# Two PSUM banks of an attention and mixture-of-experts kernel: one tile of two banks, or a tile each

## Chip, cores and metric

One core of a Trainium2 chip. The metric is the device time of one execution in microseconds (us). A measurement of this kernel can tell about 0.5% from no change.

## What is computed

Attention with random features for 4 batches, 8 heads and 576 positions gives x (2304 tokens by 512). A mixture of eight experts with Sinkhorn-balanced gates follows, and then one wide expert with a swish:

```python
out = np.zeros((N, D))                       # N = 2304, D = 512
for e in range(8):                           # first layer, F = 1024
    h = np.maximum(x @ w1[e], 0.0)
    out += P[:, e:e + 1] * (h @ w2[e])       # P: gates, 8 rounds of row and column scaling
h = out @ w_in                               # second layer, F = 2048
g = h * (1.0 / (1.0 + np.exp(-1.702 * h)))
result = g @ w_out
```

## The kernel before

The kernel first runs attention (some 210 us) and then 60 *visits*. A visit takes one block of 768 tokens (j = 0, 1, 2) through one pair of hidden chunks of 256 (c = 0, 1). There are 16 pairs of the first layer (8 experts of 2), 48 visits, and 4 pairs of the second, 12 visits. Products are made of seven smaller ones each (Strassen's scheme), and each fp32 number is two operands, a rounded one and the remainder, so a product is three matmuls.

- **Up** (`up_fast`, L1145): seven products a chunk on banks 0 to 4 and on bank 7 (`q`), six matmuls of 384 columns each (L1157), 84 in a visit. ScalarE (L1167) and VectorE (L1178, L1189, L1216) read the sums out of PSUM and form fourteen operands `h`, rounded and remainder; some of the remainders are made by GpSimd (L395).
- **Down** (`down`, L1288): DOWN (L1263) lists seven products, TURNS (L1273) their order as (n, c), PLACES (L1282) the bank and half bank of each of three token tiles t. A turn is three groups of three matmuls of 256 columns (L1302), 126 in a visit. C sits in bank 5 (both halves) and the first half of 6, E in bank 7 (both halves) and the second half of 6, D in banks 0, 2 and 1. After a turn with c = 1 the three sums are read: VectorE adds each to `acc` (L1328, L1335), or ScalarE copies it (L1318, L1324).

The two are interleaved: `all_visits` (L1383) takes the first turn of down, then the rest of up's second chunk, then the other turns; the last turn falls into the next visit. The order of the turns in both layers, the order of the token tiles t in a turn, and the banks:

```python
TURNS: (0,0), (0,1), (3,0), (1,0), (1,1), (2,0), (2,1), (3,1), (4,0), (4,1), (5,0), (5,1), (6,0), (6,1)
order = (0, 1, 2) if c == 0 else (0, 2, 1) if n == 3 else (2, 0, 1)
PLACES = {"C": ((5, 0), (5, 1), (6, 0)), "D": ((0, 0), (2, 0), (1, 0)), "E": ((7, 0), (7, 1), (6, 1))}
```

`rec` and `plan.add` (L62) collect every operation with its engine, a cost and the keys that it reads and writes. `Plan.run` (L112) then plays them through and fixes one order for each engine; an operation comes behind the last writer of each key that it touches, and a writer behind its readers too. Banks have the keys ("b", 0) to ("b", 7), one each. TensorE's main operations keep the order in which they were recorded. After that the operations are issued in this order, and semaphores between the engines are put in for each tile that two of them touch.

PSUM has eight banks of 512 fp32 columns. Banks 0 to 5 are tiles of their own. Banks 6 and 7 are the halves of one tile, PAIR (L362), because attention reads its sums of all eight heads from both banks with one instruction (`kv_step` L599, `attend` L644, `divide` L656, key PAIRS). The experts use them as `bank[6]` and `bank[7]`, views of PAIR. In the profile all that touches either of them has the name `pair`.

Of the kernel before, what the change touches and what calls it, by code (L numbers as in the profile page):

```python
# [10 lines left out]
F32 = mybir.dt.float32  # L11
# [5 lines left out]
PSUM = bass.MemoryType.PSUM  # L17
# [176 lines left out]
def tile_performer_sinkhorn_moe(  # L194
# [14 lines left out]
    nc = tc.nc  # L209
# [3 lines left out]
    E, _, F = w1.shape  # L213
    F2 = w_in.shape[1]
    P = 128
# [16 lines left out]
    Q = SUP // 2  # L232
# [3 lines left out]
    psum = ctx.enter_context(tc.tile_pool(name="psum", bufs=1, space=PSUM))  # L236
    dram = ctx.enter_context(tc.tile_pool(name="dram", bufs=1, space=bass.MemoryType.DRAM))
    plan = Plan()
# [13 lines left out]
    T = {}  # L252
# [18 lines left out]
    n = 0  # L271
# [21 lines left out]
    lg = part(SIG, "sig", 0, NTILE * E, "lg").rearrange("p (t e) -> p t e", e=E)  # L293
# [27 lines left out]
    n = H * M  # L321
# [31 lines left out]
    n = 16 * Q  # L353
# [5 lines left out]
        n += NP * P  # L359
    plan.share()  # L360

    PAIR = psum.tile([P, 2, 512], F32, name="pair")  # L362
    bank = {i: psum.tile([P, 512], F32, name=f"bank{i}") for i in range(6)}
    bank[6], bank[7] = PAIR[:, 0, :], PAIR[:, 1, :]

    scr_in = dram.tile([NC2, P, NK, FC], F32, name="scr_in")
    scr_out = dram.tile([NC2, P, NF, DM], F32, name="scr_out")
# [36 lines left out]
    def act(dur, fn, r, w):  # L404
        rec("ACT", dur, lambda e: fn(), r, w)

    def dve(dur, fn, r, w):
        rec("DVE", dur, lambda e: fn(), r, w)
# [188 lines left out]
    PAIRS = [("b", 6), ("b", 7)]  # L597

    def kv_step(b, t, f, first, last):  # L599
# [3 lines left out]
        def fn():  # L603
            for h in range(H):
                nc.tensor.matmul(
                    PAIR[:, h // 4, (h % 4) * VW : (h % 4) * VW + D + 1], f[r, h, :], vv[r, h, 0 : D + 1],
                    start=first and h % 4 == 0, stop=last, skip_group_check=True,
# [3 lines left out]
        if last:  # L611
# [4 lines left out]
                    t.rearrange("p (a h) w -> p a h w", a=2)[:, :, :, 0 : D + 1],  # L616
                    PAIR[:, :, 0 : 4 * VW].rearrange("p a (h w) -> p a h w", w=VW)[:, :, :, 0 : D + 1],
                    AF.Copy, scale=1.0 / M,
# [25 lines left out]
    def attend(ft, b):  # L644
        (ft, kf), (kx, kk) = ft, kvs[b]

        def fn():
            for h in range(H):
                nc.tensor.matmul(
                    PAIR[:, h // 4, (h % 4) * VW : (h % 4) * VW + D + 1], ft[:, h, :], kx[:, h, 0 : D + 1],  # L650
                    start=True, stop=True,
# [4 lines left out]
    def divide(x, rows):  # L656
        x, kx = x
        n = rows.stop - rows.start
        nv = PAIR[:, :, 0 : 4 * VW].rearrange("p a (h w) -> p a h w", w=VW)
        den, kd = little("den")  # L660
        rd, kr = little("rd")
        den, rd = (y.rearrange("p (a h w) -> p a h w", a=2, w=1) for y in (den, rd))
        V = nc.vector
        dve(
            0.2,
            lambda: V.tensor_scalar(
                out=den[rows], in0=nv[rows, :, :, D : D + 1], scalar1=1e-6, scalar2=None, op0=ALU.add
            ),
            PAIRS, [kd],
        )  # L670
        dve(0.2, lambda: V.reciprocal(out=rd[rows], in_=den[rows]), [kd], [kr])
        dve(
            0.69,
            lambda: V.tensor_tensor(
                out=x[rows].rearrange("p (a h d) -> p a h d", a=2, h=4), in0=nv[rows, :, :, 0:D],
                in1=rd[rows].to_broadcast([n, 2, 4, D]), op=ALU.mult,
            ),
            PAIRS + [kr], [kx],
        )
# [23 lines left out]

    def logits(j, half, b):

        lp, kp = bank[b], ("b", b)
        first, second = ((0, wg, 0), (3, wg, 2)) if half == 0 else ((1, wg, 0), (6, wgd, 0))
        n = ST // 2

        def fn():  # L710
            for a in range(2):
                for m, (o, w, at) in enumerate((first, second)):
                    for kk in range(2):
                        nc.tensor.matmul(
                            lp[0 : (2 - a) * E, :Q], w[:, at + kk, 0 : (2 - a) * E], T["xo"][o][:, a, kk],
                            start=a + m + kk == 0, stop=m + kk == 2, skip_group_check=True,
                        )

        pe(8 * MM, fn, [("xo", first[0]), ("xo", second[0]), "wg", "wgd"], [kp])
        if j == 0:  # L720
            lt, kt = T["spare"][6 + half], [("spare", 6 + half)]
        else:
            lt, kt = T["stage"][:, half * 2 * FC : half * 2 * FC + Q], [("stage", 2 * half), ("stage", 2 * half + 1)]
        act(0.5, lambda: nc.scalar.copy(lt[0 : 2 * E], lp[0 : 2 * E, :Q]), [kp], kt)

        def back():
            for t in range(n):
                nc.tensor.transpose(
                    lp[:, t * 2 * E : (t + 1) * 2 * E], lt[0 : 2 * E, t * P : (t + 1) * P],
                    ident[0 : 2 * E, 0 : 2 * E],  # L730
                )

        pe(3 * 0.11, back, kt, [kp], main=False)
        o = ST * j + n * half
        dve(
            0.3,
            lambda: nc.vector.tensor_reduce(
                out=lg[:, o : o + n, :], in_=lp[:, 0 : n * 2 * E].rearrange("p (t s e) -> p t e s", s=2, e=E),
                op=ALU.add, axis=AX.X,
            ),  # L740
            [kp], [("lg", j, half)],
        )
# [6 lines left out]
    def attention():  # L749

        seq = []
        for b in range(B):
            seq += [("k", b, t) for t in range(NT + (b + 1) % 2)]
            seq += [("q", b, t) for t in range(NT + b % 2)]
        n = len(seq)
        ins, xs = {}, {}

        def at(i, what):
            return 0 <= i < n and seq[i][0] in what

        for s in range(-5, n + 3):
            if s == n - 2:
                turn["ps"] = [4, 5]
                plan.add("X", 0.0, lambda e: switch(), (), [k for _, k in slots["b2"]] + H_KEYS)
            if at(s + 5, "kq"):
                squares(*seq[s + 5])
            if at(s + 4, "kq"):
                ins[s + 4] = project_in(*seq[s + 4])
            if at(s, "q"):
                ft = transpose_q(feat.pop(s))  # L770
            if at(s + 2, "kq"):
                pj = features(*ins.pop(s + 2))
                w, b, t = seq[s + 2]
                if w == "k" and t == NT:
                    f = ktail[b // 2] = KTAIL, "ktail"
                else:
                    i = taken("f4")
                    f = F4[i], ("f4", i)
                feat[s + 2] = f
                exps(*pj, sums.pop(seq[s + 2]), f)  # L780
            yield s - n, 0
            if at(s, "q"):
                _, b, t = seq[s]
                attend(ft, b if t < NT else b - 1)
            if at(s, "k"):
                _, b, t = seq[s]
                f = feat.pop(s)
                last = seq[s + 1][0] == "q"
                kv_step(b, t, f, t == 0, last and b % 2 == 0)
                if last and b % 2 == 1:  # L790
                    kv_step(b, NT, ktail.pop(b // 2), False, True)
            if at(s, "q"):
                _, b, t = seq[s]
                x = slot(DM, kind="sq")
                divide(x, slice(0, P if t < NT else TAIL))
                xs[s] = x
            yield s - n, 1
            if at(s - 1, "q"):
                j, t = divmod(PLACE[token_tile(*seq[s - 1][1:])], ST)
                transpose_x(xs.pop(s - 1), j, t)  # L800
            yield s - n, 2
            if at(s - 2, "q"):
                j, t = divmod(PLACE[token_tile(*seq[s - 2][1:])], ST)
                if t == ST - 1:
                    x_operands(j)
            yield s - n, 3
            if at(s, "q") and seq[s][2] == NT:
                attend(ft, seq[s][1])
                divide(x, slice(TAIL, 2 * TAIL))
            if 1 <= s < n - 8:  # L810
                load_tile(*seq[s + 8])
            if 4 <= s and at(s + 5, "k"):
                load_tile("v", *seq[s + 5][1:])
# [641 lines left out]
    with tc.manual_schedule():  # L1455
        setup()
        for t in range(NT):
            load_tile("k", 0, t)
        load_tile("k", 0, NT)
        for what, t in (("v", 0), ("v", 1), ("q", 0), ("v", 2), ("q", 1), ("v", 3), ("v", NT), ("q", 2), ("q", 3)):  # L1460
            load_tile(what, 0, t)
        load_gate()
        for c in range(2):
            prepare(0, "w1", c, 0)
            split("w1", c, 0)
        prepare(0, "w2", 0, 0)
        visits = all_visits()
        for at in attention():
            if at in EARLY:
                take(visits)  # L1470
        for _ in visits:
            pass
        for e, o in plan.run():
            o.fn(ENGINES.get(e))
        h_pool.close()


# [28 lines left out]
```

## Time and profile before

| what | value |
| --- | --- |
| device time, median of 3 runs | 2240.61 us (2237.18 to 2249.94) |
| the profiled execution: device time | 2244.87 us |
| the profiled execution: span, first to last instruction | 2243.1 us |
| mean granted TensorE clock | 0.987 |
| busy in the span: TensorE matmuls / weight loads | 2081.2 us (93%) / 1987.6 us (89%) |
| busy in the span: VectorE / ScalarE / GpSimd | 65% / 48% / 56% |

The profile is of one execution. PE is TensorE's matmuls, PEld its weight loads, DVE VectorE, ACT ScalarE, POOL GpSimd, SP the engine that issues the DMAs; L1302 is a line of the kernel. Matmuls overlap and their ends are modelled. "Idle before" is the time that an engine stood still ahead of an instruction, with what ended the wait.

### The profile page before, as it was taken

Reading aid. Unit: us, or ns where it says so; the run is one execution under the profiler, and the core shown is the slowest. Engines: PE = TensorE matmul, PEld = TensorE weight load, DVE = VectorE, ACT = ScalarE, POOL = GpSimd, SP = SyncE. Lnnn points to the kernel's source line nnn. Section 1 sums busy time; section 2 is a strip of 40 time slices with the busy share of each in tenths; the row PEclk is TensorE's granted clock in tenths of the full one; section 3 lists DMA queues with packets and bytes.
Section 4 is the critical chain, followed back from the end, with each engine's and each line's share of the span. In section 5 each row is a group of like instructions: output and inputs, shape, how many; then the busy total and the mean of one; then the engine's idle time right before and its main releaser. Section 6 shows DMA issues by size and latency. Waiting matters only on the chain. (4 is left out here: it accounts for less than half of the span.)

```text
span 2243.1 us, 39230 instructions
## 1 busy us (share of the span) xinstructions
PE 2081.2 (93%) x14191; PEld 1987.6 (89%) x14191; DVE 1455.9 (65%) x2965; ACT 1081.4 (48%) x2537; POOL 1256.1 (56%) x1215
## 2 busy tenths in 40 slices
PE   7999999999999989999999999999999879999998
PEld 7998889899898988899888889989898879898897
DVE  6874457666676675676666567656556775656755
ACT  5776553643444344344435344444534465644553
POOL 4566664756556374755547474655637253736442
PEclk8998999999999999999999999999999999999999
DMA  9545654655665564565556466545546796644542
GB/s 178 139 144 207 238 197 182 242 208 188 229 238 184 193 249 164 212 244 202 190 228 224 160 241 227 189 184 213 189 155 224 230 280 218 235 152 182 216 179 104
DMA packets 246898, 451.97 MB, mean 201 GB/s; under 512 B 73648, under 2 KB 186800, under 8 KB 246704
## 3 DMA queue, kind: packets, MB, share of 16 engines
q1 hardware_dynamic: 246704, 449.47, 57.0%
q8 instruction: 112, 1.84, 0.3%
q14 instruction: 82, 0.67, 0.1%
HBM read 403.26 MB, written 46.14 MB: 200 GB/s over the span
## 5 line engine op out<-in xcount | busy, mean ns | idle before, releaser
L1157 PE MATMUL bank<-xo,w1x 128*128 128x384 f32 x5040 | 919.2, 336 | 2.3 <-ACT ring L1167 2.2
L1157 PEld LDWEIGHTS bank<-xo,w1x 128*128 128x128 f32 x5040 | 869.7, 188 | 8.6 <-ACT ring L1167 7.6
L1302 PE MATMUL pair<-w2x,h 128*128 128x256 f32 x3600 | 564.4, 291 | 122.2 <-DVE acc L1335 68.5
L1302 PEld LDWEIGHTS pair<-w2x,h 128*128 128x128 f32 x3600 | 469.7, 188 | 191.5 <-DVE acc L1335 87.4
L1302 PE MATMUL bank<-w2x,h 128*128 128x256 f32 x3960 | 546.6, 280 | 11.5 <-DVE x2s L978 10.5
L1302 PEld LDWEIGHTS bank<-w2x,h 128*128 128x128 f32 x3960 | 502.2, 188 | 15.1 <-DVE x2s L978 11.5
L395 POOL TENSOR_TENSOR h<-ring,h 128x384 fp32r<-128x384 f32 x387 | 414.1, 1094 | 130.8 <-ACT h L1167 122.5
L395 POOL TENSOR_TENSOR w1x<-raw,w1x 128x768 fp32r<-128x768 f32 (+1 forms) x120 | 183.4, 1535 | 283.3 <-ACT w1x L1063 271.5
L1167 ACT ACTIVATE bank<-bank 128x384 f32<-128x384 f32 x120 | 57.0, 475 | 590.0 <-PE bank L1157 563.7
L1335 DVE SCALAR_TENSOR_TENSOR acc<-pair,sig,acc 128x256 f32<-128x256 f32 x378 | 170.7, 480 | 210.3 <-PE pair L1302 210.3
L395 POOL TENSOR_TENSOR raw<-raw 128x256 f32<-128x256 f32 x320 | 235.8, 763 | 92.7 <-DMA raw<-in_moe_w_dram 61.0
L1167 ACT ACTIVATE h<-ring 128x384 fp32r<-128x384 f32 x480 | 231.6, 528 | 79.8 <-DVE ring L1189 71.2
L395 POOL TENSOR_TENSOR w2x<-raw,w2x 128x768 fp32r<-128x768 f32 (+1 forms) x120 | 180.2, 1509 | 102.8 <-ACT w2x L1063 102.6
L1167 ACT ACTIVATE ring<-bank 128x384 f32<-128x384 f32 x360 | 176.2, 493 | 121.6 <-PE bank L1157 119.3
L395 POOL TENSOR_TENSOR ring<-ring 128x384 f32<-128x384 f32 (+1 forms) x106 | 109.5, 1033 | 204.6 <-ACT ring L1167 195.2
L1216 DVE SCALAR_TENSOR_TENSOR h<-bank,h 128x384 fp32r<-128x384 f32 x192 | 106.1, 554 | 156.4 <-ACT ring L1167 144.3
L1189 DVE SCALAR_TENSOR_TENSOR ring<-bank,ring 128x384 f32<-128x384 f32 x384 | 191.9, 546 | 22.6 <-PE bank L1157 21.9
L1335 DVE SCALAR_TENSOR_TENSOR acc<-bank,sig,acc 128x256 f32<-128x256 f32 x378 | 163.2, 475 | 28.5 <-PE bank L1302 28.5
L1167 ACT ACTIVATE h<-bank 128x384 fp32r<-128x384 f32 x240 | 117.3, 495 | 34.5 <-PE bank L1157 23.9
L1063 ACT CAST w2x<-raw 128x768 fp32r<-128x768 f32 (+1 forms) x120 | 82.9, 697 | 81.4 <-POOL raw L395 80.8
L1328 DVE TENSOR_TENSOR acc<-pair,acc 128x256 f32<-128x256 f32 x132 | 52.4, 421 | 88.5 <-PE pair L1302 88.1
L1063 ACT CAST w1x<-raw 128x768 fp32r<-128x768 f32 (+1 forms) x120 | 82.9, 695 | 24.0 <-PE bank L1157 14.9
(154 smaller groups left out, 2000.3 us busy)
## 6 DMA issues: line engine op xcount, KB each, us to landing
xo<-sx SPq DMA_DIRECT2D x420, 768.0 KB, 6.9
raw<-in_moe_w_dram SPq DMA_DIRECT2D x256, 128.0 KB, 4.3
sx<-x2s SPq DMA_DIRECT2D x126, 128.0 KB, 3.8
x2s<-in_moe_w_in_dram SPq DMA_DIRECT2D x16, 512.0 KB, 5.1
x2s<-in_moe_w_out_dram SPq DMA_DIRECT2D x16, 512.0 KB, 8.4
sx<-ring SPq DMA_DIRECT2D x32, 192.0 KB, 3.3
b<-in_k_dram SPq DMA_DIRECT2D x16, 256.0 KB, 4.8
b<-in_v_dram SPq DMA_DIRECT2D x16, 256.0 KB, 4.2
```

Of the source, the lines that this page charges most:

```text
L395: lambda e: e.tensor_tensor(out=out(), in0=a(), in1=b(), op=op), r, w,
L1063: lambda e, a=a, b=b: nc.scalar.copy(T[w, c, 0][:, a:b], r[:, a:b]), raws, [(w, c, g, 0)],
L1157: nc.tensor.matmul(o(b), T["w1", c, a][:, slot, kk], T["xo"][x][:, y, kk], start=start and kk == 0 and n == 0, stop=kk == 1 and n == 2, sk ...
L1167: rec("ACT", act_us(Q), lambda e: nc.scalar.activation(out(), src(), f, **kw), r, w)
L1189: lambda e: e.scalar_tensor_tensor(out=RT(out), in0=o(b), scalar=0.0, in1=RT(c), op0=ALU.max, op1=op),
L1216: lambda e: e.scalar_tensor_tensor(out=g(), in0=src[0](), scalar=0.0, in1=h().bitcast(F32), op0=ALU.max, op1=ALU.subtract),
L1302: nc.tensor.matmul(bank[i][:, u], T["h", c, a, x][:, t * P : (t + 1) * P], T["w2", c, y][:, slot], start=s and m == 0, stop=c == 1 and m = ...
L1328: lambda e, q=q, i=i, u=u: e.tensor_tensor(out=q, in0=bank[i][:, u], in1=q, op=ALU.add),
L1335: lambda e, q=q, i=i, u=u, g=g: e.scalar_tensor_tensor(out=q, in0=bank[i][:, u], scalar=g, in1=q, op0=ALU.mult, op1=ALU.add),
```

## The change

PAIR becomes a tile in a pool of its own. When attention's last operation has been issued, that pool is closed, and a second pool is opened in its place, with one tile of 512 columns for bank 6 and one for bank 7. The step (`part_pair`) is an operation of the planner without an engine and without cost, with the keys of both banks. Since the two tiles exist only from then on, `logits` looks its bank up when it is issued and not when it is recorded. Sizes, orders, keys and all instructions of the engines stay as they are.

```diff
-    PAIR = psum.tile([P, 2, 512], F32, name="pair")
     bank = {i: psum.tile([P, 512], F32, name=f"bank{i}") for i in range(6)}
-    bank[6], bank[7] = PAIR[:, 0, :], PAIR[:, 1, :]
+    pair_pool, last_pool = ExitStack(), ExitStack()
+
+    def opened_psum(stack, name):
+        return stack.enter_context(tc.tile_pool(name=name, bufs=1, reuse_waits="tile", space=PSUM))
+
+    PAIR = opened_psum(pair_pool, "pair").tile([P, 2, 512], F32, name="pair")
+
+    def part_pair():
+        pair_pool.close()
+        p = opened_psum(last_pool, "last")
+        for i in (6, 7):
+            bank[i] = p.tile([P, 512], F32, name=f"bank{i}")
...
     def logits(j, half, b):
-        lp, kp = bank[b], ("b", b)
+        kp = ("b", b)
...
-                            lp[0 : (2 - a) * E, :Q], w[:, at + kk, 0 : (2 - a) * E], T["xo"][o][:, a, kk],
+                            bank[b][0 : (2 - a) * E, :Q], w[:, at + kk, 0 : (2 - a) * E], T["xo"][o][:, a, kk],
...
             if at(s, "q") and seq[s][2] == NT:
                 attend(ft, seq[s][1])
                 divide(x, slice(TAIL, 2 * TAIL))
+            if s == n - 1:
+                plan.add("X", 0.0, lambda e: part_pair(), (), PAIRS)
...
         for e, o in plan.run():
             o.fn(ENGINES.get(e))
         h_pool.close()
+        last_pool.close()
```

## Rows read from the trace of the kernel before

**Rows 1.** The page, part 1: busy us of each engine (share of the span), instructions.

```profile
PE 2081.2 (93%) x14191; PEld 1987.6 (89%) x14191; DVE 1455.9 (65%) x2965; ACT 1081.4 (48%) x2537; POOL 1256.1 (56%) x1215
```

**Rows 2.** The page, part 5: groups of TensorE | busy us, mean ns | idle before, releaser.

```profile
L1157 PE MATMUL bank<-xo,w1x 128*128 128x384 f32 x5040 | 919.2, 336 | 2.3 <-ACT ring L1167 2.2
...
L1302 PE MATMUL pair<-w2x,h 128*128 128x256 f32 x3600 | 564.4, 291 | 122.2 <-DVE acc L1335 68.5
...
L1302 PE MATMUL bank<-w2x,h 128*128 128x256 f32 x3960 | 546.6, 280 | 11.5 <-DVE x2s L978 10.5
```

**Rows 3.** Waits of TensorE in the whole span: us in total, times, longest us.

```profile
PE pair L1302 <- DVE acc L1335: 68.5, 141, 0.7
PE pair L1302 <- DVE acc L1328: 15.6, 31, 0.6
PE pair L1302 <- ACT ring L1167: 12.4, 38, 1.3
PE pair L1302 <- ACT bank L1318: 11.1, 19, 3.1
PE bank L1302 <- DVE x2s L978: 10.5, 3, 5.3
...
PE pair L1302 <- DVE h L1216: 4.6, 6, 2.4
...
PE pair L1302 <- DVE h L1178: 3.2, 6, 0.6
...
PE pair L1302 <- ACT acc L1324: 2.3, 7, 0.5
...
PE pair L1302 <- ACT h L1167: 1.2, 5, 0.4
```

**Rows 4.** Timeline of TensorE in one visit: start us, us, instructions xcount [idle before].

```profile
1127.49 0.62 PE L1302 MATMUL pair<-w2x,h 128*128 128x256 f32 x3 [0.19 <-ACT ring L1167]
1127.95 1.21 PE L1157 MATMUL bank<-xo,w1x 128*128 128x384 f32 x6
...
1131.29 2.99 PE L1302 MATMUL bank<-w2x,h 128*128 128x256 f32 x24
...
1135.57 1.32 PE L1302 MATMUL pair<-w2x,h 128*128 128x256 f32 x9
...
1138.25 0.98 PE L1302 MATMUL pair<-w2x,h 128*128 128x256 f32 x6 [0.61 <-DVE acc L1335]
...
1139.80 2.02 PE L1302 MATMUL pair<-w2x,h 128*128 128x256 f32 x15
1142.40 0.62 PE L1302 MATMUL pair<-w2x,h 128*128 128x256 f32 x3 [0.58 <-DVE acc L1335]
...
1144.00 0.62 PE L1302 MATMUL pair<-w2x,h 128*128 128x256 f32 x3 [0.27 <-DVE acc L1335]
```

**Rows 5.** Timeline of VectorE in the same visit.

```profile
1128.21 0.56 DVE L1216 SCALAR_TENSOR_TENSOR h<-pair,h 128x384 fp32r<-128x384 f32 x1 [1.02 <-PE pair L1302]
...
1136.93 1.26 DVE L1335 SCALAR_TENSOR_TENSOR acc<-pair,sig,acc 128x256 f32<-128x256 f32 x3 [0.32 <-PE pair L1302]
...
1141.87 0.48 DVE L1335 SCALAR_TENSOR_TENSOR acc<-pair,sig,acc 128x256 f32<-128x256 f32 x1 [1.02 <-PE pair L1302]
1143.07 0.88 DVE L1335 SCALAR_TENSOR_TENSOR acc<-pair,sig,acc 128x256 f32<-128x256 f32 x2 [0.72 <-PE pair L1302]
```

**Rows 6.** Windows: stretch, length, busy us of each engine, granted clock, DMA share, GB/s.

```profile
228.20:1756.80 1528.60, 1438.11 (x9741) 1376.24 (x9739) 991.31 (x1995) 675.91 (x1498) 895.52 (x840) 1.00 0.56 206
...
1126.40:1159.00 32.60, 30.95 (x212) 29.88 (x211) 21.12 (x45) 11.42 (x28) 16.31 (x19) 1.00 0.56 214
596.00:629.30 33.30, 31.15 (x212) 29.66 (x212) 23.09 (x46) 16.16 (x35) 27.28 (x25) 1.00 0.63 227
1804.50:1807.90 3.40, 3.40 (x15) 3.40 (x15) 3.12 (x5) 1.16 (x4) 3.40 (x4) 0.50 1.00 382
```

More of the change, by code (lines that the diff above doesn't have):

```diff
@@ L723, in logits @@
             lt, kt = T["stage"][:, half * 2 * FC : half * 2 * FC + Q], [("stage", 2 * half), ("stage", 2 * half + 1)]
-        act(0.5, lambda: nc.scalar.copy(lt[0 : 2 * E], lp[0 : 2 * E, :Q]), [kp], kt)
+        act(0.5, lambda: nc.scalar.copy(lt[0 : 2 * E], bank[b][0 : 2 * E, :Q]), [kp], kt)
         def back():
@@ L728, in back @@
                 nc.tensor.transpose(
-                    lp[:, t * 2 * E : (t + 1) * 2 * E], lt[0 : 2 * E, t * P : (t + 1) * P],
+                    bank[b][:, t * 2 * E : (t + 1) * 2 * E], lt[0 : 2 * E, t * P : (t + 1) * P],
                     ident[0 : 2 * E, 0 : 2 * E],
@@ L737, in logits @@
             lambda: nc.vector.tensor_reduce(
-                out=lg[:, o : o + n, :], in_=lp[:, 0 : n * 2 * E].rearrange("p (t s e) -> p t e s", s=2, e=E),
+                out=lg[:, o : o + n, :], in_=bank[b][:, 0 : n * 2 * E].rearrange("p (t s e) -> p t e s", s=2, e=E),
                 op=ALU.add, axis=AX.X,
```

## Prediction

> **What bounds the kernel now.** I read the page first. TensorE's matmul row is busy 2081.2 us of 2243.1, more than any other engine [rows 1], so the question is what fills its 162 idle microseconds, and whether "busy" hides more. The groups by line answer the first part [rows 2]: the 5040 products of the up stage (L1157) have 2.3 us of idle time ahead of them, the 3960 down products into banks with tiles of their own 11.5 us, and the 3600 down products into `pair` 122.2 us. The same instruction on the same line waits ten times as long when its target is called `pair`. The waits of TensorE [rows 3] say on whom: on VectorE's additions out of PSUM into `acc` (L1335, L1328), on ScalarE's and VectorE's reads of bank 7 for the operand `h` (L1167, L1216, L1178), and on ScalarE's copies out of bank 6 (L1318).
>
> Then one visit, the 28th of 60 (1126.4 to 1159.0 us), TensorE beside VectorE [rows 4, 5]. With the code's orders each matmul can be given its bank: `down` walks TURNS, three matmuls a group, and PLACES says where. The row of 15 matmuls on `pair` from 1139.80 is turn (5,0), banks 7, 7, 6, and then turn (5,1), bank 6 and the first half of 7; the three left over, the second half of bank 7, start at 1142.40 after 0.58 us of idle time, on VectorE. What was VectorE doing? Its read at 1141.87 began only when the 15 had ended, although bank 6 was complete three matmuls sooner. It can only be the read of bank 6: the planner's keys let no read of bank 7 start before bank 7's last matmul. So a read of bank 6 waited for matmuls into bank 7, and a matmul into bank 7 waited for that read. The same holds at 1138.25: six matmuls into bank 6 wait until three reads (1136.93 to 1138.19) have ended, only one of which reads bank 6. And at 1144.00: bank 6 waits for a read of bank 7. The visible order is kept over the tile, not over the bank.
>
> **The change, part by part.** No instruction is added to or taken from an engine; the planner's keys ("b", 6) and ("b", 7) were separate before, so its order on each engine stays. What goes are waits between two banks.
>
> Price of one wait. The idle time in the list is not the whole price. A down matmul shows as 280 ns [rows 2], but 24 in a row take 2.99 us [rows 4], so they follow each other at (2.99-0.28)/23 = 0.118 us: the first 0.16 us after the last start is hidden under a modelled end. And a row of three after a wait lasts 0.62 us, against 0.28 + 2 x 0.118 = 0.52 without one: 0.10 us more. So a wait costs its idle time plus 0.26 us. The Trainium skill (Perfetto Trace Analysis, Identifying the Most-Contended Engine) holds that busy time of matmuls is a poor measure of headroom since they are pipelined, and that the busy time of weight loads is the good one; the row agrees, with 255.5 us not busy on weight loads against 161.9 on matmuls [rows 1]. By matmul idle time alone the sum below would be some 105 us in place of 187.
>
> What replaces the waits, in that visit [rows 4, 5]. The three matmuls of 1142.40 are issued by 1142.40 + 0.10 + 3 x 0.118 = 1142.85, and their reads start at 1143.07: 0.2 us. A read runs 0.48 us (0.40 apart in a row). The reads that end at 1138.19 release the row of 1138.25: 0.06. Together 0.74 us, while a group of three takes 0.35.
> - The first bank 6 write (0.19 idle, on ScalarE's read of bank 7) starts at once. The next write to bank 7 is one group, six up products (1.05 us) and three groups later, 2.4 us, by when those reads are over; VectorE's own read at 1128.21, itself 1.02 us late behind bank 6's matmuls, comes forward.
> - The row at 1138.25 (0.61): bank 6's read follows its own three matmuls, not the next three, so it starts 0.35 us sooner and is over some 0.3 us before TensorE wants the bank.
> - The row at 1142.40 (0.58) needs nothing: bank 7's last reads ended at 1138.19.
> - The row at 1144.00 (0.27) needs bank 6's read, which ends two groups sooner.
> What is late next is bank 5: its first write of turn (4,0) comes 0.2 us after VectorE's read of it can end (three reads 0.40 us apart; the last is over 1.19 us after the last group of turn (2,1) starts, and the write comes 4 x 0.35 = 1.41 after it), the smallest margin in this visit.
>
> The sum, from the waits [rows 3]:
> - (a) reads of sums, L1335, L1328, L1324: 179 waits, 86.4 us, and 179 x 0.26 = 46.5: 133. All go, by the visit above.
> - (b) reads of bank 7 for `h`: 55 waits, 21.4 us, and 14.3: 36. In the 48 visits of the first layer they go; in the last 12 the swish lengthens that chain and the true wait, a bank 7 write three groups on, remains in part. I take 30.
> - (c) ScalarE's copies of bank 6, L1318: 19 waits, 11.1 us, and 4.9: 16. The copy is a true reader of bank 6, which the third group after it writes; only the bank 7 groups ahead of it were held for nothing. The longest, 3.1 us, is a late ScalarE and stays. I take 6, between 0 and 13.
> - (d) waits under 0.15 us, which the list does not name. A visit's 84 up matmuls (5040 in 60) at (1.21-0.335)/5 = 0.175 [rows 4] and 126 down ones (7560 in 60) at 0.118 make 29.5 of its 32.6 us; 3.1 are lost. The four named waits are 1.65 us (which is 32.60 less the 30.95 busy, [rows 6]) plus 4 x 0.26, 2.7; 0.4 a visit is left, over 57 visits 23. I take 18.
> - Not touched: the three waits on y's operands, L978, 10.5 us, and the whole of attention, whose tile stays as it is.
> - Closing attention's pool: the new tiles wait for the old one's last reader, as bank 6 and 7's next writers did before. Nothing, or at most one more wait like the longest on `pair`, 3.1 us.
>
> Together 133 + 30 + 6 + 18 = 187; the most is 133 + 36 + 13 + 23 = 205. The profiled execution took 2244.87 us (span 2243.1); less 187 is 2058, less 205 is 2040. The runs' median is 4.3 us below that execution, so I say 2053 for the median.
>
> Cover. Every visit gets about 3.1 us shorter of 33, so what the other engines do per visit must fit into 30. VectorE is busy 21.1 us in the visit shown, and GpSimd 27.3 us in the visit that splits the next weights [rows 6], so that one has 3 us to spare. The DMA engines at a share of 0.56 go to 0.62. All fit, GpSimd barely; what it leaves over falls into the next visits, like the one shown, where it has 16.3 us of work.
>
> **The rivals.**
> - New waits take half of it. If VectorE, in order, reaches the reads of bank 5 and 6 half a microsecond later than above, or GpSimd's operands come late in its full visits, the margin of 0.2 us is gone and TensorE stops in other places. For it: GpSimd's 27.3 of 33.3 us. Against: the up products wait only 2.3 us in all [rows 2], so weights and x operands are not near their limit. Price: half of the sum, 94 us, 2147.
> - Nothing happens, because the stalls are true ones: bank 6 holds parts of both C and E and is soon written again, which is in the rows as well. Then 2240. The Trainium skill (Perfetto Trace Analysis, Optimization Strategy) says that a bubble that repeats on the engine that should be full can mean too little PSUM, which splitting a tile cannot mend; all eight banks are indeed taken. Against, without the page: the three rows above, where the waiting bank is not the one read.
> - Slower, by TensorE's clock. If the denser stream were answered by a lower granted clock, each microsecond would do less. The row of 1804.5 to 1807.9 us shows the lower level: granted 0.50 (1.2 GHz), 15 matmuls in 3.40 us, 0.23 us each, where the visit makes 212 in 30.95, 0.146 each [rows 6]: 0.36 of the time is lost. The 187 us are cancelled when 187/0.36 = 520 us of the span run so; with 560 us it would be 2053 + 202 = 2255. Against: that stretch follows one of the three stops on L978, of up to 5.3 us [rows 3], while through 1528.6 us of visits at 94% busy the clock was 1.00 [rows 6]. The change makes stops shorter.
>
> **How the numbers follow.** 0.76 for the forecast, 0.16 for half, 0.05 for nothing, 0.03 for slower. The forecast's own range is 2030 (205 us, less the 4.3, and a few us of L978) to 2085 (with (b) to (d) lost). To leave out no more than 0.2 I reach into the half case: 2024 to 2122. A measurement here tells 0.5%, 11 us, from no change: faster 0.76 + 0.16 = 0.92, same 0.05, slower 0.03.
>
> **What would show it.** Right: the idle time ahead of down products into banks 6 and 7 falls from 122.2 us to under 20, the waits on L1335 and L1328 almost vanish, a first-layer visit takes 29.5 to 30.0 us, and three matmuls after the row of 15 follow without a gap, while VectorE's read of bank 6 starts 0.2 us after its own three. Wrong: the same idle time under other names, waits on GpSimd's `h` or on L1328's reads of bank 5; or granted clock under 1.00 in 300 to 1750 us; or visits still at 32.6.

## The result and the profile after

| kernel | device time, median (lowest to highest) | ratio to before |
| --- | --- | --- |
| before | 2242.79 us (2237.18 to 2249.94) | 1 |
| changed | 2067.65 us (2065.20 to 2075.01) | 0.9223 [0.9186, 0.9260] |

The change takes off 175 us, 7.8%. The forecast was 2053; it lies 15 us below. The profiled execution of the changed kernel took 2075.01 us, with a span of 2073.2: 170 less than before, where 187 were forecast.

The order of the instructions on each engine is the same in both traces, and so are their counts. First the page of the changed kernel, part 1, busy us of each engine:

```profile
PE 2007.5 (97%) x14191; PEld 1971.0 (95%) x14191; DVE 1474.2 (71%) x2965; ACT 1080.6 (52%) x2537; POOL 1270.5 (61%) x1215
```

And its part 5, TensorE's two groups of the experts (busy us, mean ns, idle before, releaser). L1314 is L1302 of before, L1169 is L1157; the name `pair` is gone from the down products.

```profile
L1314 PE MATMUL bank<-w2x,h 128*128 128x256 f32 x7560 | 939.3, 281 | 32.4 <-DVE acc L1347 12.8
...
L1169 PE MATMUL bank<-xo,w1x 128*128 128x384 f32 x5040 | 919.7, 337 | 4.6 <-ACT ring L1179 3.8
```

The 7560 down products have 32.4 us of idle time ahead of them, where it was 122.2 + 11.5 [rows 2]. Matmul idle time as a whole fell by 96 us (161.9 to 65.7), the time by 170. The Trainium skill (Perfetto Trace Analysis, Identifying the Most-Contended Engine) has weight loads as the truer measure of TensorE, and the two pages agree: time not busy on weight loads fell from 255.5 to 102.2, by 153.

The waits of TensorE in the whole span, longest total first (us in total, times, longest us; L1347 and L1340 are L1335 and L1328 of before, L990 is L978, L1330 is L1318):

```profile
PE bank L1314 <- DVE acc L1347: 12.8, 18, 1.1
PE bank L1314 <- DVE x2s L990: 9.9, 2, 6.2
...
PE bank L1169 <- ACT ring L1179: 3.8, 3, 2.5
PE bank L1314 <- DVE h L1190: 3.6, 5, 1.1
...
PE bank L1314 <- ACT bank L1330: 3.0, 2, 2.8
...
PE bank L1314 <- DVE acc L1340: 1.8, 4, 0.7
```

Of the 172 waits on VectorE's two lines of additions [rows 3], 22 are left. The 38 waits of down products on ScalarE's reads of bank 7 (L1167) no longer stand among the first ten, and those on the copies of bank 6 went from 19 to 2, a long one still there.

TensorE in the visit of [rows 4] (start us, us, instructions):

```profile
1053.75 1.22 PE L1314 MATMUL bank<-w2x,h 128*128 128x256 f32 x9
1054.81 1.20 PE L1169 MATMUL bank<-xo,w1x 128*128 128x384 f32 x6
1055.85 12.96 PE L1314 MATMUL bank<-w2x,h 128*128 128x256 f32 x108
```

What was broken into rows of 24, 9, 6, 15, 3 and 3 with waits between is now one row of 108 matmuls, at (12.96 - 0.28)/107 = 0.1185 us each: close to the 0.118 that the prediction took from the best row of before. VectorE under it, against [rows 5]:

```profile
1061.65 0.48 DVE L1347 SCALAR_TENSOR_TENSOR acc<-bank,sig,acc 128x256 f32<-128x256 f32 x1 [0.78 <-PE bank L1314]
1062.35 2.05 DVE L1347 SCALAR_TENSOR_TENSOR acc<-bank,sig,acc 128x256 f32<-128x256 f32 x5 [0.22 <-PE bank L1314]
1064.99 0.48 DVE L1347 SCALAR_TENSOR_TENSOR acc<-bank,sig,acc 128x256 f32<-128x256 f32 x1 [0.59 <-PE bank L1314]
1065.69 0.88 DVE L1347 SCALAR_TENSOR_TENSOR acc<-bank,sig,acc 128x256 f32<-128x256 f32 x2 [0.22 <-PE bank L1314]
1067.09 0.48 DVE L1347 SCALAR_TENSOR_TENSOR acc<-bank,sig,acc 128x256 f32<-128x256 f32 x1 [0.52 <-PE bank L1314]
1067.79 0.88 DVE L1347 SCALAR_TENSOR_TENSOR acc<-bank,sig,acc 128x256 f32<-128x256 f32 x2 [0.22 <-PE bank L1314]
```

The last two rows are the sums of turn (5,1), whose reads stood at 1141.87 and 1143.07 in [rows 5]. By the order of the code TensorE's three matmuls into bank 6 start from 1066.54 on and those into bank 7 from 1066.89 on. The read of bank 6 starts at 1067.09, 0.2 us after its own three, and the two of bank 7 follow after a pause of 0.22 us; the read no longer waits for bank 7. The rows before them are turns whose next bank is bank 5, a tile of its own in both kernels. One thing there is not as the prediction had it. The read at 1062.35 comes 0.70 us after the one before, which is two groups of 0.35: bank 5's first half is read only when both halves are complete.

The windows of the changed kernel (stretch, us, busy us of PE, PEld, DVE, ACT, POOL with counts, granted clock, DMA share, GB/s): the first 46 visits, the three with the operands of the second layer, the rest, and then two single visits, the 28th (to be set beside 32.60 in [rows 6]) and a third visit of a pair of chunks (j = 2, beside 33.30).

```profile
231.80:1630.10 1398.30, 1380.05 (x9740) 1360.29 (x9739) 1009.97 (x1996) 674.21 (x1500) 907.74 (x840) 1.00 0.62 226
1630.10:1746.60 116.50, 101.47 (x687) 99.19 (x687) 90.13 (x190) 70.21 (x177) 58.65 (x57) 0.94 0.91 286
1746.60:2073.20 326.60, 316.80 (x2234) 311.60 (x2232) 217.29 (x469) 184.73 (x427) 174.14 (x165) 1.00 0.53 196
1053.75:1083.20 29.45, 29.45 (x211) 29.33 (x211) 21.11 (x45) 11.47 (x28) 16.26 (x19) 1.00 0.63 231
662.31:692.70 30.39, 29.66 (x211) 29.34 (x211) 23.95 (x45) 16.02 (x35) 27.40 (x25) 1.00 0.71 249
```

The first 46 visits went from 1528.6 to 1398.3 us (130.3, or 2.83 a visit), the three with y's operands from 125.2 to 116.5 (8.7), the rest from 361.1 to 326.6 (34.5): 173.5 in all. What lies ahead of the first visit took 3.6 us more; that stage spread from 220.9 to 232 us over the profiles of all kernels below, so the 3.6 is within that spread. The 28th visit is 29.45 us long and TensorE busy for all of it. The third visit has 0.73 us of idle time in it, and here is that place, first TensorE, then VectorE and GpSimd:

```profile
664.40 6.82 PE L1314 MATMUL bank<-w2x,h 128*128 128x256 f32 x57
671.95 0.74 PE L1314 MATMUL bank<-w2x,h 128*128 128x256 f32 x4 [0.73 <-DVE acc L1347]
```

```profile
665.63 1.94 DVE L1201 SCALAR_TENSOR_TENSOR ring<-bank,ring 128x384 f32<-128x384 f32 x4
667.49 2.83 DVE L405 TENSOR_TENSOR h<-ring,h 128x384 fp32r<-128x384 f32 x2
670.25 2.43 DVE L1347 SCALAR_TENSOR_TENSOR acc<-bank,sig,acc 128x256 f32<-128x256 f32 x6
```

```profile
666.07 2.55 POOL L405 TENSOR_TENSOR w1x<-raw,w1x 128x512 fp32r<-128x512 f32 x2
668.58 2.62 POOL L405 TENSOR_TENSOR h<-ring,h 128x384 fp32r<-128x384 f32 x2
```

VectorE makes two operand remainders (L405, L395 of before) ahead of its reads, with GpSimd at work beside it. They take 2.83 us, 1.42 each; the planner's cost for one is 1.01. The reads start late and without a pause. The 57 matmuls end with the first group of turn (3,1), so what TensorE waits for is bank 6: the fourth of the six reads, that of bank 6 for turn (2,1), ends at 670.25 + 3 x 0.40 + 0.48 = 671.93.

### The profile page after: what moved, and what is told of

Its sections match the earlier page's. It is cut to its first block, busy times and chain, and to the rows that moved or that the text cites. A ratio compares the mean times of both kernels' runs of the same rounds, so it can differ in the third digit from the quotient of the medians.

```text
span 2073.2 us, 39087 instructions
## 1 busy us (share of the span) xinstructions
PE 2007.5 (97%) x14191; PEld 1971.0 (95%) x14191; DVE 1474.2 (71%) x2965; ACT 1080.6 (52%) x2537; POOL 1270.5 (61%) x1215
## 4 chain that ended last, share of the span: by engine, by line
PE 78%; DVE 13%; ACT 3%; DMA 2%; issue 1%; POOL 0%; SPq 0%; DVEq 0%; ACTq 0%; POOLq 0%
PE bank L1169 37%; PE bank L1314 35%; DVE ring L1201 2%; DVE h L405 2%; DMA sx<-x2s 2%; DVE acc L1347 1%; PE pair L659 1%; PE pair L615 1%; DVE bank L1190 1%; ACT acc L602 1%; ACT h L1179 1%; PE bank L566 1%; DVE h L1228 1%; DVE x2s L990 1%; PE bank L642 1%
## 5 line engine op out<-in xcount | busy, mean ns | idle before, releaser
L1314 PE MATMUL bank<-w2x,h 128*128 128x256 f32 x7560 | 939.3, 281 | 32.4 <-DVE acc L1347 12.8
L1314 PEld LDWEIGHTS bank<-w2x,h 128*128 128x128 f32 x7560 | 917.3, 189 | 47.5 <-DVE acc L1347 17.3
L1169 PE MATMUL bank<-xo,w1x 128*128 128x384 f32 x5040 | 919.7, 337 | 4.6 <-ACT ring L1179 3.8
L1169 PEld LDWEIGHTS bank<-xo,w1x 128*128 128x128 f32 x5040 | 869.8, 189 | 11.5 <-ACT ring L1179 9.7
L405 POOL TENSOR_TENSOR h<-ring,h 128x384 fp32r<-128x384 f32 x387 | 421.0, 1114 | 100.2 <-ACT h L1179 98.2
L1347 DVE SCALAR_TENSOR_TENSOR acc<-bank,sig,acc 128x256 f32<-128x256 f32 x756 | 328.2, 477 | 134.9 <-PE bank L1314 134.2
L405 POOL TENSOR_TENSOR w1x<-raw,w1x 128x768 fp32r<-128x768 f32 (+1 forms) x120 | 182.6, 1528 | 250.9 <-ACT w1x L1075 240.5
L405 POOL TENSOR_TENSOR raw<-raw 128x256 f32<-128x256 f32 x320 | 241.9, 781 | 100.4 <-DMA raw<-in_moe_w_dram 66.4
L1179 ACT ACTIVATE ring<-bank 128x384 f32<-128x384 f32 x480 | 233.2, 491 | 123.0 <-PE bank L1169 118.7
L1228 DVE SCALAR_TENSOR_TENSOR h<-bank,h 128x384 fp32r<-128x384 f32 x288 | 158.9, 554 | 172.4 <-ACT ring L1179 159.5
L405 POOL TENSOR_TENSOR w2x<-raw,w2x 128x768 fp32r<-128x768 f32 (+1 forms) x120 | 180.7, 1514 | 52.8 <-ACT w2x L1075 52.3
L1179 ACT ACTIVATE h<-bank 128x384 fp32r<-128x384 f32 x360 | 176.1, 494 | 69.6 <-DVE bank L1190 44.5
L405 POOL TENSOR_TENSOR ring<-ring 128x384 f32<-128x384 f32 (+1 forms) x106 | 111.1, 1049 | 150.1 <-ACT ring L1179 138.8
L1190 DVE TENSOR_TENSOR bank<-bank,ring 128x384 f32<-128x384 f32 x240 | 133.6, 560 | 39.4 <-PE bank L1169 38.3
L1340 DVE TENSOR_TENSOR acc<-bank,acc 128x256 f32<-128x256 f32 x252 | 95.6, 418 | 59.2 <-PE bank L1314 58.3
L405 DVE TENSOR_TENSOR h<-ring,h 128x384 fp32r<-128x384 f32 x93 | 96.4, 1048 | 1.4 <-ACT h L1179 1.1
L602 ACT ACTIVATE acc<-bank,acc 128x128 f32<-128x128 f32 x272 | 77.0, 401 | 26.0 <-DVE acc L595 19.0
```

Of the source, the lines that this page charges most:

```text
L405: lambda e: e.tensor_tensor(out=out(), in0=a(), in1=b(), op=op), r, w,
L602: lambda h=h, pv=pv: nc.scalar.activation(f[:, h, :], pv[:, h % 4, :], AF.Exp, bias=nb[:, h : h + 1]),
L1169: nc.tensor.matmul(o(b), T["w1", c, a][:, slot, kk], T["xo"][x][:, y, kk], start=start and kk == 0 and n == 0, stop=kk == 1 and n == 2, sk ...
L1179: rec("ACT", act_us(Q), lambda e: nc.scalar.activation(out(), src(), f, **kw), r, w)
L1190: lambda e: e.tensor_tensor(out=out[0](), in0=a[0](), in1=b[0](), op=op), [a[1], b[1]], [out[1]],
L1228: lambda e: e.scalar_tensor_tensor(out=g(), in0=src[0](), scalar=0.0, in1=h().bitcast(F32), op0=ALU.max, op1=ALU.subtract),
```

## The experiments

The theory: the lost time is waits between two banks that share a tile, and of what was forecast but did not come, most lies in bank 5 and in a VectorE that is late. The rivals: that something else in the edit gained the time (pools closed and opened, addresses looked up at issue), that the reads themselves cost it, or that the shortfall is noise. The kernel before, run beside the experiments, had medians of 2245 to 2247 us; the ratios are to these. Two runs stand for the changed kernel: 2067.65 above, and again beside the second set, 2067.60 (2064.94 to 2072.79; 0.9207 [0.9188, 0.9226]):

> The changed kernel once more, beside the three below on the same chip: 2068 us (2060 to 2076).

**The edit with one tile again.** The pool is closed and reopened at the same place, but with one tile of both banks.

```diff
-        p = opened_psum(last_pool, "last")
-        for i in (6, 7):
-            bank[i] = p.tile([P, 512], F32, name=f"bank{i}")
+        both = opened_psum(last_pool, "last").tile([P, 2, 512], F32, name="pair")
+        bank[6], bank[7] = both[:, 0, :], both[:, 1, :]
```

> Attention's pool is closed and reopened as in the changed kernel, but what is opened is one tile of two banks again. If the time came from waits between bank 6 and bank 7, all of it is lost: 2243 us (2230 to 2255), and TensorE idles about 120 us ahead of down products on this tile, on L1335 and L1328 above all. If the new pool, its place in PSUM or the later look-up of the bank brought it, the time stays near 2068.

Measured: 2246.81 us, ratio 1.0007 [0.9991, 1.0022]. Its waits of TensorE:

```profile
PE pair L1313 <- DVE acc L1346: 68.9, 141, 0.8
PE pair L1313 <- DVE acc L1339: 15.8, 32, 0.6
```

The waits of [rows 3] are back, 141 and 32 for 141 and 31, and the order on each engine is that of the changed kernel. So the whole gain, 2246.81 - 2067.65 = 179 us, hangs on the number of tiles, and the closing of the pool costs and gains nothing that can be measured.

**Without the reads of banks 6 and 7, with one tile and with two.** VectorE's additions out of these two banks are left out, so that the output lacks those sums; the matmuls and ScalarE's copies stay.

```diff
+                elif i in (6, 7):
+                    pass
                 elif l or e == 0:
```

> One tile of two banks, and VectorE leaves out its additions of the sums of banks 6 and 7 into acc (the copies of the first visits stay). If these reads were the largest term, 133 us, the time is 2243 - 133 = 2110 (2095 to 2130) although the banks share a tile. If the term was smaller and the stalls come from the shared tile in other ways, over 2160.

> The same additions left out with two tiles, in the same order of operations as with one. What the changed kernel still waits for on VectorE's additions is 14.6 us in 22 waits, with 0.26 us each 20 us: 2068 - 20 = 2048 (2040 to 2058). Against the run with one tile the difference is what is left of the shared tile's waits, on h and on ScalarE's copies: 45 to 65 us. If VectorE, freed of 500 additions, frees nothing, 2068.

One tile: 2101.69 us, 0.9340 [0.9317, 0.9363]; two tiles: 2058.40, 0.9153 [0.9129, 0.9177]. TensorE's waits with one tile:

```profile
PE pair L1313 <- ACT bank L1329: 9.2, 14, 3.1
PE pair L1313 <- ACT ring L1178: 9.1, 31, 0.6
PE pair L1313 <- DVE h L1227: 6.2, 16, 0.5
```

and with two:

```profile
PE bank L1314 <- DVE acc L1349: 9.6, 17, 0.9
```

With one tile the additions cost 2246.81 - 2101.69 = 145 us, with two 2067.65 - 2058.40 = 9. A read of a bank is thus nearly free, and what was paid is its standing in one tile with the next bank. What is left with one tile, 43 us above two, is on the other readers of bank 7 and on the copies, terms (b) to (d) of the prediction. The 9 us were expected to be 20: 17 waits stay with these additions left out, and all are ahead of the first write to bank 5 in turn (4,0).

**The operand's bank 7 put into bank 6.** Bank 7 holds no product of up: VectorE puts a sum there (L1178 of before), which the readers for `h` take. Here there are two tiles, but that sum is made in bank 6, between the same neighbours. It overwrites what lies there, so `h` and the output are of other numbers.

```diff
         def o(b):
-            return bank[b][:, :Q]
+            return bank[6 if b == 7 else b][:, :Q]
```

> Two tiles as in the changed kernel and the same order of operations, but the sums that up keeps in bank 7 lie in bank 6, ahead of whose readers down's first group writes it (so the operand of these sums is made of overwritten data). This brings back the waits on bank 7's readers alone, the term that the prediction priced at 36 us and took as 30. By that theory 2068 + 25 to 40 = 2093 to 2108, with waits of groups in bank 6 on ScalarE's and VectorE's reads for h, and no new ones on the additions into acc. If these waits lay beside others and cost nothing, under 2078.

Measured: 2098.49 us, 0.9333 [0.9315, 0.9350]: 31 us more than the changed kernel. Its waits:

```profile
PE bank L1314 <- ACT ring L1179: 11.8, 37, 1.3
...
PE bank L1314 <- DVE h L1228: 5.2, 7, 2.4
```

The wait for ScalarE's read is back with 37 times and 11.8 us, where [rows 3] had 38 and 12.4. Counted as in the last part, turns (0,0) and (0,1) lose 49.9 us, 37 more than in the changed kernel, while turns (3,1) and (4,0) lose 5 less, so the 31 is a net figure. Term (b) alone was taken at 30.

**Bank 6 first in turn (3,1).** Of the turns with c = 1 and sums in bank 6, this one alone takes bank 6 second, between the two halves of bank 7. The edit puts bank 6 first, as in the others. The planner's order on the other engines shifts a little with it.

```diff
-            order = (0, 1, 2) if c == 0 else (0, 2, 1) if n == 3 else (2, 0, 1)
+            order = (0, 1, 2) if c == 0 else (2, 0, 1)
```

> In turn (3,1) the group in bank 6 goes first, as in the other turns. Then it follows VectorE's true reading of bank 6 at 0.70 us where that takes 0.74: a wait of 0.04 and its 0.10 in each visit, and 0.35 us more in the visits where VectorE is late, every third. Against it, turn (4,0) begins that much later and its wait on bank 5 (0.08 and 0.11 a visit) becomes shorter. If 0.74 us is the right price of a true reader, the two nearly cancel: 2068 to 2080, with short waits ahead of turn (3,1) in every visit. If a true reader cost nothing at this distance, 2055 to 2062.

Measured: 2070.44 us (2063.36 to 2078.36), 0.9225 [0.9203, 0.9247], beside the changed kernel's 0.9207: no difference that can be told. Its waits and a third visit of it, where the second row begins turn (3,1) with bank 6:

```profile
PE bank L1314 <- DVE acc L1347: 16.3, 23, 1.4
```

```profile
654.13 6.46 PE L1314 MATMUL bank<-w2x,h 128*128 128x256 f32 x54
661.81 6.54 PE L1314 MATMUL bank<-w2x,h 128*128 128x256 f32 x54 [1.22 <-DVE acc L1347]
```

Taken over all visits, from start to start of the matmuls (the way of counting stands in the last part), the time lost in turn (3,1) rose from 12.7 to 28.8 us, and that in turn (4,0), which begins with the first write to bank 5, fell from 15.7 to 3.9. The margin is moved from one bank to the other. So the small loss ahead of bank 5 is a true dependence, of the order of the tiles, and no remnant of the old coupling.

**VectorE made less late, in two ways.** In the first the remainders of `h` go to GpSimd always; in the second they may go to either, but the planner reckons VectorE's cost at 0.17 + 0.0033 a column (1.44 us for 384), near the 1.42 measured; in the third both.

```diff
-                tt(g, src[0], lambda: h().bitcast(F32), ALU.subtract, Q, [src[1], hk], [gk])
+                tt(g, src[0], lambda: h().bitcast(F32), ALU.subtract, Q, [src[1], hk], [gk], eng="POOL")
...
-        return {"DVE": dve_us(n), "POOL": 0.27 + 0.0022 * n}
+        return {"DVE": 0.17 + 0.0033 * n, "POOL": 0.27 + 0.0022 * n}
```

> The remainders of operands made from ring tiles go to GpSimd alone (VectorE made 93 of them, 1.05 us each and up to 1.55, and in every third visit two of these stand ahead of its reads of the sums). If VectorE's lateness behind them is what is left in these visits (waits on its additions, 12.8 us in 18 waits), they vanish: 2068 - 12 to 18 = 2050 to 2056. The rival: GpSimd, busy 27 of 31 us in these visits, makes them later still, and TensorE waits on GpSimd's h: 2068 or more.

> The planner reckons such an operation on VectorE with 1.44 us for 384 columns in place of 1.01 (the trace has 1.0 to 1.55 when GpSimd runs beside it), so it places reads of sums and remainders with a truer price. If the plan's price is why VectorE comes late, 2052 to 2062; if the lateness is a matter of the amount of work in these visits and not of its order, 2064 to 2074.

> Both: the remainders on GpSimd alone, and 1.44 us in the plan for such an operation on VectorE. If both mend the same thing, VectorE's lateness ahead of its reads of sums, there is little left to gain: 2040 to 2052, as with either alone (2047 and 2052). If the two gains were of different waits they add up: 2030 to 2037.

Measured: 2046.76 us (0.9119 [0.9099, 0.9139]) on GpSimd, 2051.92 (0.9134 [0.9114, 0.9153]) by the price, 2049.87 (0.9136 [0.9115, 0.9157]) with both. That is 21, 16 and 18 us off the changed kernel; the three can't be told apart, and both edits together are worth what one is. The waits of the first:

```profile
PE bank L1314 <- DVE acc L1347: 3.6, 7, 0.9
```

and its engines:

```profile
PE 2004.2 (98%) x14191; PEld 1968.8 (96%) x14191; DVE 1409.8 (69%) x2888; ACT 1079.7 (53%) x2537; POOL 1325.1 (64%) x1292
```

In the balance 77 instructions went from VectorE to GpSimd. The waits on the additions fell from 18 to 7, the mean third visit (14 of them, between the fourth visit of all and the 45th) from 30.75 to 29.91 us, and GpSimd, with 55 us more work, did not come late. This is the fastest kernel of the study: nearly 200 us under before.

**The same in the kernel before.** Does the late VectorE cost as much while the banks are one tile?

> The kernel before, with one tile of both banks, and the remainders on GpSimd alone. With the shared tile TensorE waits for VectorE's reads in every visit whether VectorE is late or not; in the visits where it is late, 11 and 16 us of the idle time come from it at most. If its lateness is mostly hidden under the shared tile's waits, 2246 - 0 to 10 = 2236 to 2246; if it costs there what it costs with two tiles, 21 us, 2225.

```profile
PE pair L1302 <- DVE acc L1335: 65.5, 133, 0.7
```

Measured: 2231.44 us, 0.9950 [0.9930, 0.9970], 7 to 16 us off, a little more than expected. 133 of the 141 waits stay. By the medians 14 of the 21 us that the same edit gains with two tiles are gained here too: most of VectorE's lateness is older than the change. Whether the rest was covered by the old waits and came into the open when they went, the intervals are too wide to say.

## Why the prediction was right, and where it was 15 us off

**What bounds it.** Right. The waits were between two banks of one tile. One tile in the same pool gives 2246.81 us, two give 2067.65, and nothing else differs: the order on each engine is the same.

**The price of a wait** (idle time and 0.26 us). Right. VectorE's two lines have 172 waits with 84.1 us of idle time before [rows 3]. With 0.26 each they are worth 129, without it 84; leaving the reads of these two banks out gave 145. The changed visit's row of 108 at 0.1185 us bears out the interval from which the 0.26 was made.

**The terms**, as far as experiments add up:

| term | taken | measured | how |
| --- | --- | --- | --- |
| (a) reads of sums | 133 | 136 | 145 with one tile less 9 with two (ScalarE's 7 copies of sums stay) |
| (b) reads of bank 7 for `h` | 30 | 31 | operand put into bank 6 |
| (c) and (d) copies, short waits | 24 | 12 | 179 - 136 - 31 |
| sum | 187 | 179 | one tile against two |

The first two agree within 3 us, closer than the medians can show: by the intervals each is known to some 5 us, so the 12 of the last two, a rest of three differences, can be 10 off. The traces say more. The time from the start of one matmul to the next, less what it is in a row without stops (median 0.117 us after a down product, 0.174 after an up product), is what TensorE loses; added up by turn over all 60 visits, in us:

| turns | before | changed |
| --- | --- | --- |
| (0,0) and (0,1), behind reads of bank 7 for `h` (the stops on y's operands, some 10, in both) | 49.4 | 12.6 |
| (3,0), behind the copies of bank 6 | 24.3 | 10.4 |
| (3,1) to (6,0), behind the reads of sums | 159.1 | 28.2 |
| all else | 19.5 | 26.7 |

The first two rows gain 37 and 14, more than the 30 and 6 taken for (b) and (c). The third gains 131 of its 159, where the prediction said of (a) "All go, by the visit above": 28 us stay, 12.7 in turn (3,1) and 15.7 in turn (4,0). That is the step that fell short; all else loses 7 more. Together the gain is 174, and the windows above have 173.5.

**The mis-sized step** under it is the one on what is late next: "bank 5: its first write of turn (4,0) comes 0.2 us after VectorE's read of it can end". The place was right, the margin was not. I had let the read of bank 5's first half start when that half was complete. It starts behind both halves, as the row at 1062.35 shows, for the planner's key is the bank. So the two reads end 0.20 + 0.40 + 0.48 + 0.06 = 1.14 us after the last group of the turn, and the write comes three groups, 1.05 us, after it: a wait of 0.09 us in place of 0.2 us of slack. The trace has 0.08 us there in 25 first-layer visits, and 0.11 more at the restart; it is below what the list of waits names. In nine more visits VectorE is late and the stop 0.2 to 1.1 us long. In most third visits the late VectorE stops TensorE earlier, at bank 6 in turn (3,1): 12 stops of 0.4 to 0.9 us, 11 of them in third visits. The fourth experiment could move these losses but not take them away. The sum explains 8 of the 15 us (187 for 179). The rest is its starting point: the forecast was counted from 2240.6 us, and the kernel before ran at 2245 to 2247 beside the experiments.

**Cover.** "All fit, GpSimd barely" was half right. GpSimd fitted, with 27.40 of 30.39 us busy in the third visit shown. VectorE was the one that came late, with 23.95 busy: not for want of time in the visit, but since two subtractions of 1.42 us stood ahead of its reads. Taking them away gave 21 us back, the better part of it in third visits (14 of them by 0.84 us, 12 us); in the kernel before, the same gave 14.

**The rivals.** "New waits take half" was true in kind (VectorE late, bank 5's margin gone) at some 28 us, not 94. "Nothing" fell with the result. "Slower by the clock" fell with the windows: behind attention the granted clock was 1.00 through the first 46 visits at 99% busy, and under it, at 0.94, only in the stage of the stops on L990.

**What would show it.** 29.5 to 30.0 us a first-layer visit: 29.45 in the one shown, means by j of 29.6, 30.0 and 30.75 from the fourth visit to the 45th, so the third visits missed it; with the first three and the 46th the mean is 1398.3/46 = 30.4. Under 20 us of idle time ahead of products into banks 6 and 7: the page can't tell the banks apart any more, but by the order of the code 16.4 of the 32.4 us are ahead of these two. The row of 15 with three behind it is inside the 108. The second layer keeps a true wait, as said: the 5 waits on L1190, up to 1.1 us, four of them ahead of bank 7 in turn (3,0); its visit (mean of the last ten whole ones) went from 33.62 to 30.45.

**Open.** How the short waits of (d) share out among the turns, and how much of VectorE's lateness the kernel before already paid: 7 to 16 us, of the 21 that it costs with two tiles.

## What to carry to other kernels

Where one engine's instructions wait ten times as long on one tile as on its neighbours of the same line, look which bank the waiting instruction writes and which one the releaser reads: if they differ, the tile is too coarse, and splitting it costs no instruction. Price such waits by the restart as well as by the idle time, which here more than doubled some of them. Then look for the next reader with a margin of a few tenths of a microsecond, counting its start from the unit that the order is kept on, and for what stands ahead of it on its engine.

## What the runs showed of the hardware

The same VectorE subtraction of two operands from SBUF, 128x384 with a rounded result, took 0.54 to 1.69 us in the changed kernel. Its group with all durations of the 93 (ns, min/median/max, first and last start):

```profile
L405 DVE TENSOR_TENSOR h<-ring,h x93: 542/1032/1686, 236.8 to 2057.2; 128x384 fp32r<-128x384 f32 x93
```

The long ones shown above had GpSimd at work through all of their time. Over the 93, the four with GpSimd at work for less than half of their time took 0.55 us, and the 73 with it at work for over 90% took 0.55 to 1.69, median 1.07: none was long without GpSimd, but some were short beside it. That GpSimd's traffic is what stretches them is the likely reading, but it is not shown, as no run took it away by itself. The additions out of PSUM on the same engine kept their length, with GpSimd at work or idle: 0.48 us at a mean of 477 ns over 756.
